# Sharing PSUM banks between a DFT filter and its inverse, and joining eight mixer loops into one, in an fp32 GFNet and MLP-mixer kernel

## The chip, the cores and the metric

The kernel runs on one core of a Trainium2 chip. The metric is the device time of one execution in microseconds. The profile comes from one execution of its own, and its times are read against that execution's span.

## The reference, cut to what matters

The input has 8 batches of 3008 rows by 256 columns, all in fp32. Per batch, a filter in the frequency domain along the rows comes first, then an MLP mixer over the rows (tokens) and one over the columns (channels):

```python
X = np.fft.rfft(x, axis=1)
Y = X * (filt_r + 1j * filt_i)[None, :, :]
x = np.fft.irfft(Y, n=3008, axis=1)
xt = x.transpose(0, 2, 1)
h = np.maximum(xt @ w_tok1, 0.0) @ w_tok2      # 3008 -> 256 -> 3008
u = x + h.transpose(0, 2, 1)
h2 = np.maximum(u @ w_ch1, 0.0) @ w_ch2        # 256 -> 1536 -> 256
out = u + h2
```

## The kernel before, in words

Four stages follow each other for each batch, and stages of different batches run beside each other.

- **Filter, first half** (`a_unit`, lines 376 to 381). The DFT of 3008 = 47 x 64 points is split in two. A unit loads two columns of x, multiplies by a 128x128 table on TensorE (L378), copies the 128x512 result out of PSUM on ScalarE (L380) and stores it to `z_tmp` in device memory (L381). There are 12 units in a batch.
- **Filter, second half** (`b_unit` and `bi_unit`, lines 408 to 444). For each of 32 steps k, `b_unit` multiplies by the second table (L410) into a bank, and VectorE multiplies that bank by the filter (L423, L424, L425 read the bank, L427 adds two products in SBUF). `bi_unit` then applies the inverse table (L434), ScalarE copies the result out (L439), and it is stored to `g_tmp` (L444). In step k the order is: `b_unit(k)`, then `bi_unit(k - 1)`.
- **Token mixer** (`token_sums`, L471; `token_relu`, L477; `u_unit`, L488 to L495). 48 matmuls make the hidden layer of 256. A `u_unit` makes one half of a 512-row tile of u by matmuls with the second weights, adds the end of the inverse DFT (L493), and ScalarE copies it out (L495).
- **Channel mixer** (`mix`, lines 634 to 694). A batch has six row tiles, m, and in each six pairs of hidden blocks, jp: 36 items. The two matrix products use seven block products instead of eight, with sums on VectorE (all recorded on L506). `up_first` (L528, with a ScalarE copy, L531) and `up_last` (L544) make the hidden values in two `pg` banks, VectorE adds them up into hh, ScalarE applies the relu (L549), and `down` in two parts (L562) adds to four banks, po0 to po3. `down` of item i - 1 stands beside `up` of item i. So the loop over a batch has a 37th turn, which has `down` alone. After the last jp of a tile `finish` (lines 565 to 609) gives six steps of VectorE work and stores, which `one_step` takes up one at a time.

PSUM has eight banks: four `po`, two `pg`, and one each named `acc` and `b`. Beside the mixer, `a_unit` and `b_unit` write `b`, and `bi_unit`, `token_sums` and `u_unit` write `acc`. Only in the start, before any mixer runs, are the banks taken differently (`first`).

The order is written out by hand: each engine does its instructions in the order in which the program gives them. `mix` is a generator that stops at three places in each item: after the first part of `down`, place 0; after `up_last`, place 1; and at the item's end, place 2. At these places the loop at lines 733 to 747 puts in one step of `dft`, the filter of the next group of batches. The groups are (0), (1, 2), (3, 4), (5, 6), (7). Beside a group of two batches one step goes in at place 1 of each item. Beside batch 0, which is alone, the 24 first-half units go in at all three places, and the second-half steps at place 1 and in two items of three at place 2. The mixer weights of the channel part are converted on VectorE in the first items of batch 0 (L216 to L242, called by `convert`).

In an item, `u_unit` of the next tile stands at jp 3 and 4, between the second part of `down` and place 2. Near a batch's end (item 32) come the next batch's `token_sums`, then its first two `u_unit`s. `loads` fetches `g_tmp` for the next batch (tile `t4`) when the filter of that batch is done (`next_ready`).

Of the kernel before, what the change touches and what calls it, by code (L numbers as in the profile page):

```python
# [17 lines left out]
B = 8  # L18
# [18 lines left out]
TC = DT // P  # L37
DC = 1536
JT = DC // P
JP = JT // 2  # L40
# [3 lines left out]
MT = 6  # L44
# [73 lines left out]
def kernel(  # L118
# [44 lines left out]

    def bank(tag):
        return (psg if tag == "pg" else psum).tile([P, 512], FP32, tag=tag, name="ps_" + tag)

    wa = glob.tile([P, P], FP32, name="wa")
    wai = glob.tile([P, P], FP32, name="wai")
# [204 lines left out]
    def rows_of(t_d, b):  # L373
        return t_d[b].rearrange("k (g a) d -> (k g) a d", a=A)

    def a_unit(b, c, tag):
        ps = bank(tag)
        nc.tensor.matmul(ps, wa, xs.pop((b, c)).rearrange("p a d -> p (a d)"), start=True, stop=True)  # L378
        t1 = t1p.tile([P, XC, D], FP32, tag="t1", name="t1")
        nc.scalar.copy(out=t1.rearrange("p a d -> p (a d)"), in_=ps)  # L380
        nc.scalar.dma_start(rows_of(z_d, b)[:, ts(c, XC), :], t1)  # L381

    def dft(bs):
        first = bs[0] == 0
        nb = len(bs)
        todo = [(b, c) for b in bs for c in range(NXC)]
        ahead = 3 * XB if first else XB
        for u in todo[0:ahead]:
            x_load(*u)
        for i, u in enumerate(todo):  # L390
            a_unit(*u, ("acc", "b")[i % 2] if first else "b")
            if i + ahead < len(todo):
                x_load(*todo[i + ahead])
            yield i + 1 < len(todo)
        wbs, t2s, t3s, prods = {}, {}, {}, {}

        def load(c):
            if c * KC % WC == 0:
                g = c * KC // WC
                wbs[g] = wbp.tile([P, WC, P + KR], FP32, tag="wb", name="wb")  # L400
                nc.sync.dma_start(wbs[g], wbi_d[:, ts(g, WC), :])
            filt_load(c, (nc.sync, nc.gpsimd, nc.gpsimd) if first else (nc.sync,) * 3)
            where, tag = (sp, "s") if first and c % 3 == 2 else (t2p, "t2")
            t2s[c] = where.tile([KR, KC, nb, D], FP32, tag=tag, name="t2")
            for i, b in enumerate(bs):
                nc.sync.dma_start(t2s[c][:, :, i, :], z_d[b, ts(c, KC)].rearrange("k r d -> r k d"))

        def b_unit(k):
            ps = bank(("b", "pg")[k % 2] if first else "b").rearrange("p (b d) -> p b d", b=2)[:, 0:nb, :]
            nc.tensor.matmul(ps, wbs[k // WC][0:KR, k % WC, 0:P], t2s[k // KC][:, k % KC],  # L410
                             start=True, stop=True)
            re, im = slice(0, HALF), slice(HALF, P)
            t = filts[k // KC % FB]
            fr = t[:, 0, k % KC, :].unsqueeze(1).to_broadcast([P, nb, D])
            fi = t[im, 1, k % KC, :].unsqueeze(1).to_broadcast([HALF, nb, D])
            p1 = p1p.tile([P, 2 if first else nb, D], FP32, tag="p1", name="p1")
            if first:
                p1, p2 = p1[:, 0:1], p1[:, 1:2]
                prods[k] = (p1, p2)
            else:  # L420
                p2 = p2p.tile([P, nb, D], FP32, tag="p2", name="p2")
                prods[k] = (p1,)
            nc.vector.tensor_tensor(out=p1, in0=ps, in1=fr, op=ALU.mult)  # L423
            nc.vector.scalar_tensor_tensor(out=p2[re], in0=ps[im], scalar=-1.0, in1=fi, op0=ALU.mult, op1=ALU.mult)  # L424
            nc.vector.tensor_tensor(out=p2[im], in0=ps[re], in1=fi, op=ALU.mult)  # L425
            if not first:
                nc.vector.tensor_tensor(out=p1, in0=p1, in1=p2, op=ALU.add)  # L427

        def bi_unit(k):

            ps = bank("acc").rearrange("p (b d) -> p b d", b=2)[:, 0:nb, :]
            parts = prods.pop(k)
            for i, p in enumerate(parts):
                nc.tensor.matmul(ps[0:KR], wbs[k // WC][:, k % WC, P:], p, start=(i == 0), stop=(i == len(parts) - 1))  # L434
            c, r = divmod(k, KC)
            if r == 0:
                t3s[c] = t3p.tile([KR, KC, nb, D], FP32, tag="t3", name="t3")

            nc.scalar.copy(out=t3s[c][:, r].rearrange("p b (e g i) -> p b g e i", e=DH, i=CW),  # L439
                           in_=ps[0:KR].rearrange("p b (g e i) -> p b g e i", e=DH, i=CW))  # L440
            if r == KC - 1:
                t3 = t3s.pop(c)
                for i, b in enumerate(bs):
                    nc.scalar.dma_start(g_d[b, ts(c, KC)].rearrange("k r d -> r k d"), t3[:, :, i, :])  # L444

        load(0)
        load(1)
        yield
        yield
        for k in range(K2 + 1):  # L450
            if k < K2:
                b_unit(k)
                if k % KC == 0 and k // KC + 2 < K2 // KC:
                    load(k // KC + 2)
            if k >= 1:
                bi_unit(k - 1)
            yield
# [7 lines left out]
        nc.sync.dma_start(t4[b, c], rows_of(g_d, b)[:, ts(c, TC4), :])  # L465

    def token_sums(b):
        acc = bank("acc").rearrange("p (t d) -> p t d", t=TC)
        for a in range(A):
            for t in range(TC):  # L470
                nc.tensor.matmul(acc[:, t, :], w1[:, a, ts(t, P)], t4[b, a // TC4][:, a % TC4, :],  # L471
                                 start=(a == 0 and t == 0), stop=(a == A - 1 and t == TC - 1))
        return acc
# [9 lines left out]
    def u_unit(b, m, h1, ut, dh):  # L483

        w = width(m)
        ps = bank("acc")
        for t in range(TC):
            nc.tensor.matmul(ps[:, 0:w], h1[:, t, ts(dh, P)], w2[:, t, ds(m * 512, w)],  # L488
                             start=(t == 0), stop=False)
# [138 lines left out]
    todo_v = []  # L628
# [2 lines left out]
        if todo_v:  # L631
            todo_v.pop(0)()

    def mix(b, next_ready):

        wait = [0]
        pos, hhs, tts = {}, {}, {}
        more = b + 1 < B

        def loads():  # L640
            if more and next_ready():
                for c in wait:
                    t4_load(b + 1, c)
                wait.clear()

        items = [(m, jp) for m in range(MT) for jp in range(JP)]
        n = len(items)
        for i in range(n + 1):
            now, old = i < n, i >= 1
            convert()  # L650
            if now:
                m, jp = items[i]
                w = width(m)
                hhs[i] = hp.tile([P, 4, 256], FP32, tag="hh", name="hh")
                g = [bank("pg").rearrange("p (s n) -> p s n", s=2) for _ in range(2)]
                s = up_first(jp, uts[b, m], vts[b, m], w, g)
                up_middle(hhs[i], w, g, s)
            one_step()
            if old:
                mo, jo = items[i - 1]  # L660
                tts[i - 1] = tp.tile([P, 4, 256], FP32, tag="t", name="t")
                for f in h_sums(hhs[i - 1], tts[i - 1], width(mo)):
                    f()
                down(mo, jo, 0, hhs[i - 1], tts[i - 1], pos.setdefault(mo, []))
            yield i, 0
            convert()
            if now:
                up_last(jp, uts[b, m], vts[b, m], w, g, s, hhs[i])
            one_step()
            loads()  # L670
            yield i, 1
            if old:
                down(mo, jo, 1, hhs.pop(i - 1), tts.pop(i - 1), pos[mo])
                if jo == JP - 1:
                    todo_v.extend(finish(b, mo, uts[b, mo], pos[mo]))
                    one_step()
                    one_step()
            if now:
                if m + 1 < MT and jp in (3, 4):
                    u_part(b, m + 1, jp - 3)  # L680
                    if jp == 4:
                        wait.append(m + 1)
                        todo_v.extend(v_steps(b, m + 1))
                if more and i == n - 4:
                    h1s[b + 1] = token_relu(token_sums(b + 1))
                if more and n - 3 <= i < n - 1:
                    u_part(b + 1, 0, i - n + 3)
                    if i == n - 2:
                        todo_v.extend(v_steps(b + 1, 0))
            loads()  # L690
            yield i, 2
        if not more:
            while todo_v:
                one_step()

    with tc.manual_schedule():
        nc.sync.dma_start(wa, wa_d)
# [32 lines left out]
            u_part(0, 0, dh)  # L730
        for f in v_steps(0, 0):
            f()
        for bs, after in zip(GROUPS, GROUPS[1:] + ((),)):
            todo = dft(after) if after else iter(())
            done = not after
            spread = True
            for b in bs:
                def next_ready():
                    return b != bs[-1] or done

                for i, place in mix(b, next_ready):

                    if not done and (place == 1 or bs == GROUPS[0] and (spread or place == 2 and i % 3)):
                        spread = next(todo, "end")
                        done = spread == "end"
            for _ in todo:
                raise AssertionError("the filter's steps don't fit beside the mixer's")


# [28 lines left out]
```

## Time and profile before

| | |
|---|---|
| time, median of three runs | 2620.95 us |
| the three runs | 2620.94, 2620.95, 2629.69 us |
| span of the profiled execution | 2619.4 us (that execution's time: 2621.18 us) |
| mean granted TensorE clock | 0.986 |
| start, before the first channel mixer item | to about 181 us |
| batch 0's mixer, with the filter of batches 1 and 2 beside it | 181 to 557 us |
| a 128x256 matmul of L562, start to start | 0.43 us |
| ScalarE copies of 128x512 | L495 586 ns, L380 572 ns |
| VectorE sum of 128x512 out of PSUM (hh, L506) | 682 ns |

A row of the waits reads: the engine and line that waited, the engine and line that it waited for, the total, how often, and the longest. In the order of time, the number in brackets is how long the engine had been idle, with what ended the idle time. PE is TensorE's matmuls, DVE is VectorE, ACT is ScalarE. An instruction that is recorded as x2 is one fp32 matmul in two records.

### The profile page before, as it was taken

How to read it: one execution, taken by the hardware profiler on the slowest of the kernel's cores; microseconds unless marked ns; L12 is line 12 of the kernel's file. 1: busy time of each engine (PE TensorE's matmuls, PEld its weight loads, DVE VectorE, ACT ScalarE, POOL GpSimd, SP SyncE). 2: the span in 40 equal slices, each digit the busy share in tenths (PEclk: the TensorE clock that was granted, in tenths of full speed). 3: DMA queues.
4: the chain of work that ended last, by engine and by line, in shares of the span. 5: the costliest groups of instructions: out<-in, count | busy, mean ns of one | idle time of the engine just before them, and what ended most of it. 6: DMA issues, size and time to landing. Idle time of an engine off the chain costs nothing.

```text
span 2619.4 us, 31533 instructions
## 1 busy us (share of the span) xinstructions
PE 2513.3 (96%) x10928; PEld 2000.7 (76%) x10928; DVE 1804.4 (69%) x3461; ACT 678.9 (26%) x1325; POOL 519.3 (20%) x951
## 2 busy tenths in 40 slices
PE   6869999999999999999999999999999999999998
PEld 2446666788878777888787777788888888888887
DVE  3787788645666888646567688745678586647676
ACT  2223222222321222213222222212222122212222
POOL 3534111211121111211212111121121121211212
PEclk7879999999999999999999999999999999999999
DMA  8765433312232332202332222211322111100001
GB/s 235 221 192 177 123 111 111 103 42 89 85 100 63 88 89 61 87 9 90 95 101 85 74 82 75 75 33 56 95 77 84 54 46 55 25 9 8 17 10 22
DMA packets 158104, 212.89 MB, mean 81 GB/s; under 512 B 35012, under 2 KB 106383, under 8 KB 157945
## 3 DMA queue, kind: packets, MB, share of 16 engines
q1 hardware_dynamic: 85897, 120.34, 15.7%
q0 software_dynamic: 30656, 39.92, 6.2%
q10 hardware_dynamic: 41392, 50.62, 5.7%
q8 instruction: 86, 1.41, 0.2%
q14 instruction: 73, 0.60, 0.1%
HBM read 135.77 MB, written 74.97 MB: 80 GB/s over the span
## 4 chain that ended last, share of the span: by engine, by line
PE 74%; DVE 14%; issue 2%; ACT 1%; DMA 0%; DVEq 0%; SPq 0%; POOL 0%; ACTq 0%; POOLq 0%
PE ps_po L562 26%; PE ps_pg L528 15%; PE ps_pg L544 11%; PE ps_acc L488 6%; PE ps_acc L471 6%; PE ps_acc L493 3%; DVE t L506 3%; DVE hh L506 3%; PE ps_b L410 3%; PE ps_b L378 2%; PE ps_acc L434 2%; DVE u L506 2%; DVE s L506 1%; DVE p L425 1%; DVE p L424 1%
## 5 line engine op out<-in xcount | busy, mean ns | idle before, releaser
L506 DVE TENSOR_TENSOR hh<-ps_pg,s 128x512 f32<-128x512 f32 (+3 forms) x864 | 482.8, 586 | 643.8 <-ACT s L531 643.2
L607 POOL DMA_DIRECT2D out_dram<-r x757 | 409.8, 550 | 1964.7 <-ACT hh L549 893.9
L549 ACT ACTIVATE hh<-hh 128x512 f32<-128x512 f32 (+1 forms) x576 | 348.0, 621 | 1103.0 <-DVE hh L506 1103.0
L562 PE MATMUL ps_po<-t,wc 128*128 128x256 f32 (+1 forms) x2304 | 535.5, 375 | 3.5 <-DVE t L506 2.2
L562 PEld LDWEIGHTS ps_po<-t,wc 128*128 128x128 f32 x2304 | 434.4, 190 | 127.6 <-issue 50.8
L562 PE MATMUL ps_po<-hh,wc 128*128 128x256 f32 (+1 forms) x1728 | 413.1, 375 | 3.1 <-ACT hh L549 3.1
L528 PE MATMUL ps_pg<-v,wc 128*128 128x256 f32 (+1 forms) x1728 | 414.1, 376 | 1.6 <-DVE v L506 1.6
L562 PEld LDWEIGHTS ps_po<-hh,wc 128*128 128x128 f32 x1728 | 327.4, 190 | 42.4 <-ACT hh L549 5.1
L528 PEld LDWEIGHTS ps_pg<-v,wc 128*128 128x128 f32 x1728 | 327.6, 190 | 41.7 <-DVE v L506 2.3
L544 PE MATMUL ps_pg<-u,wc 128*128 128x256 f32 (+1 forms) x1152 | 294.1, 378 | 9.6 <-DVE hh L506 9.3
L506 DVE TENSOR_TENSOR t<-t,hh 128x256 f32<-128x256 f32 (+1 forms) x576 | 242.9, 422 | 19.8
L544 PEld LDWEIGHTS ps_pg<-u,wc 128*128 128x128 f32 x1152 | 215.3, 190 | 49.2 <-DVE hh L506 22.3
L506 DVE TENSOR_TENSOR s<-ps_pg,hh 128x512 f32<-128x512 f32 (+1 forms) x288 | 196.1, 681 | 30.6 <-DVE hh L506 0.5
L506 DVE TENSOR_TENSOR t<-hh 128x512 f32<-128x512 f32 (+1 forms) x288 | 192.5, 668 | 0.6 <-ACT hh L549 0.6
L488 PE MATMUL ps_acc<-w,h 128*128 128x512 f32 (+1 forms) x384 | 181.7, 596 | 7.7 <-ACT h L477 3.5
L471 PE MATMUL ps_acc<-t,w 128*128 128x256 f32 x768 | 170.3, 384 | 8.0 <-DMA t<-g_tmp 6.7
L528 PE MATMUL ps_pg<-u,wc 128*128 128x256 f32 (+1 forms) x576 | 170.3, 377 | 0.4 <-DVE hh L506 0.4
L471 PEld LDWEIGHTS ps_acc<-t,w 128*128 128x128 f32 x768 | 147.5, 193 | 29.8 <-issue 7.1
L544 PE MATMUL ps_pg<-v,wc 128*128 128x256 f32 (+1 forms) x576 | 168.9, 375 | 0.0
L410 PE MATMUL ps_b<-t,wb 96*128 96x512 f32 (+1 forms) x288 | 130.3, 533 | 31.8 <-DMA t<-z_tmp 17.6
L434 PE MATMUL ps_acc<-p,wb 128*96 128x256 f32 (+1 forms) x384 | 154.7, 497 | 2.4 <-DVE p L423 1.1
L531 ACT COPY s<-ps_pg 128x256 f32<-128x256 f32 (+1 forms) x288 | 106.0, 368 | 152.0 <-PE ps_pg L528 147.4
(71 smaller groups left out, 1954.2 us busy)
## 6 DMA issues: line engine op xcount, KB each, us to landing
z_tmp<-t ACTq DMA_DIRECT2D x96, 256.0 KB
t<-z_tmp SPq DMA_DIRECT2D x128, 192.0 KB
g_tmp<-t ACTq DMA_DIRECT2D x128, 192.0 KB
t<-g_tmp SPq DMA_DIRECT2D x48, 512.0 KB
x<-in_x_dram SPq DMA_DIRECT2D x184, 128.0 KB
out_dram<-r POOLq DMA_DIRECT2D x698, 32.0 KB, 1.8
wb<-wbi_t SPq DMA_DIRECT2D x80, 224.0 KB
filt<-in_filt_r_dram SPq DMA_DIRECT2D x144, 48.0 KB
```

Of the source, the lines that this page charges most:

```text
L410: nc.tensor.matmul(ps, wbs[k // WC][0:KR, k % WC, 0:P], t2s[k // KC][:, k % KC], start=True, stop=True)
L434: nc.tensor.matmul(ps[0:KR], wbs[k // WC][:, k % WC, P:], p, start=(i == 0), stop=(i == len(parts) - 1))
L471: nc.tensor.matmul(acc[:, t, :], w1[:, a, ts(t, P)], t4[b, a // TC4][:, a % TC4, :], start=(a == 0 and t == 0), stop=(a == A - 1 and t == ...
L488: nc.tensor.matmul(ps[:, 0:w], h1[:, t, ts(dh, P)], w2[:, t, ds(m * 512, w)], start=(t == 0), stop=False)
L493: nc.tensor.matmul(ps[:, ds(q * P, n)], t4[b, c][:, r, ts(dh, P)], wai[:, 0:n], start=False, stop=(q == 3))
L506: nc.vector.tensor_tensor(out=out, in0=in0, in1=in1, op=op)
L528: nc.tensor.matmul(ps[:, 0:hw], wc1[:, jp, n, :], mov, start=True, stop=True)
L531: nc.scalar.copy(out=s[:, 0], in_=g[0][:, 0, 0:hw])
L544: nc.tensor.matmul(ps[:, 0:hw], wc1[:, jp, n, :], mov, start=True, stop=True)
L549: nc.scalar.activation(out=hs, in_=hs, func=AF.Relu)
L562: nc.tensor.matmul(po[i][:, j, 0:hw], wc2[:, jp, n, :], mov, start=(jp == 0 and first == 1), stop=(jp == JP - 1 and last == 1))
L607: q.dma_start(rows[g, e, :, ds(h * A + 4 * m, n)], blocks[ts(g, CW), h, e, 0:n])
```

## The change

It has two parts.

**Banks.** A helper `free_bank` gives acc and b in turn, except that it passes over a bank that is held. `a_unit`, `token_sums` and `u_unit` all take their bank from it. Beside the mixer `b_unit(k)` takes its bank from it too and holds it; `bi_unit(k)` writes its result into the same bank, over the product that VectorE has read by then, and the hold ends. So the product and the inverse of one step share a bank, and at most one bank is held while something else asks. In the start `b_unit` and `bi_unit` keep their banks, while `a_unit`, `token_sums` and `u_unit` take turns there too.

**One sequence.** `mix` runs once over 288 items of all eight batches, not eight times over 36. The 37th turn of seven batches goes: `down` of a batch's last item stands beside `up` of the next batch's first item. The loop at the end becomes one loop, which starts the next group's `dft` when the first item of a group is reached.

The diff, cut to its core:

```diff
+    turn, held = ["acc", "b"], []
+
+    def free_bank():
+        turn.reverse()
+        if turn[0] in held:
+            turn.reverse()
+        return turn[0]
...
-    def a_unit(b, c, tag):
-        ps = bank(tag)
+    def a_unit(b, c):
+        ps = bank(free_bank())
...
-            a_unit(*u, ("acc", "b")[i % 2] if first else "b")
+            a_unit(*u)
...
-            ps = bank(("b", "pg")[k % 2] if first else "b").rearrange("p (b d) -> p b d", b=2)[:, 0:nb, :]
+            tag = ("b", "pg")[k % 2] if first else free_bank()
+            if not first:
+                held.append(tag)
+            ps = bank(tag).rearrange("p (b d) -> p b d", b=2)[:, 0:nb, :]
...
-            ps = bank("acc").rearrange("p (b d) -> p b d", b=2)[:, 0:nb, :]
+            ps = bank("acc" if first else held.pop(0)).rearrange("p (b d) -> p b d", b=2)[:, 0:nb, :]
...
-        acc = bank("acc").rearrange("p (t d) -> p t d", t=TC)
+        acc = bank(free_bank()).rearrange("p (t d) -> p t d", t=TC)
...
-        ps = bank("acc")
+        ps = bank(free_bank())
...
-    def mix(b, next_ready):
-
-        wait = [0]
+    def mix(next_ready):
+
+        wait = []
...
-        items = [(m, jp) for m in range(MT) for jp in range(JP)]
-        n = len(items)
-        for i in range(n + 1):
-            now, old = i < n, i >= 1
+        items = [(b, m, jp) for b in range(B) for m in range(MT) for jp in range(JP)]
+        n = MT * JP
+        for i in range(len(items) + 1):
+            now, old = i < len(items), i >= 1
             convert()
             if now:
-                m, jp = items[i]
+                b, m, jp = items[i]
+                if i % n == 0:
+                    wait.append(0)
...
-        for bs, after in zip(GROUPS, GROUPS[1:] + ((),)):
-            todo = dft(after) if after else iter(())
...
-                for i, place in mix(b, next_ready):
-
-                    if not done and (place == 1 or bs == GROUPS[0] and (spread or place == 2 and i % 3)):
-                        spread = next(todo, "end")
-                        done = spread == "end"
...
+        for b, i, place in mix(next_ready):
+            if group + 1 < len(GROUPS) and b == GROUPS[group + 1][0]:
+                if not done:
+                    raise AssertionError("the filter's steps don't fit beside the mixer's")
+                group += 1
+                done = group + 1 == len(GROUPS)
+                todo = iter(()) if done else dft(GROUPS[group + 1])
+                spread = True
+
+            if not done and (place == 1 or group == 0 and (spread or place == 2 and i % 3)):
+                spread = next(todo, "end")
+                done = spread == "end"
```

## The prediction

> **What bounds the kernel now.** First the page's span and busy times, then the busy times by stage. The columns of the second view are the stretch and its length, busy us and instructions of each engine, granted TensorE clock, DMA share and GB/s; the stages are the start, the mixer of batch 0 up to 453 us, the steady part, the end.
>
> ```profile
> span 2619.4 us, 31533 instructions
> PE 2513.3 (96%) x10928; PEld 2000.7 (76%) x10928; DVE 1804.4 (69%) x3461; ACT 678.9 (26%) x1325; POOL 519.3 (20%) x951
> ```
>
> ```profile
> 0.00:167.00 167.00, 121.02 (x360) 69.93 (x360) 107.37 (x233) 42.79 (x86) 70.91 (x133) 0.85 0.80 234
> 167.00:453.00 286.00, 257.03 (x980) 179.37 (x981) 231.32 (x410) 81.70 (x152) 64.64 (x109) 0.97 0.43 128
> 453.00:2566.00 2113.00, 2092.63 (x9372) 1711.28 (x9371) 1429.72 (x2745) 542.92 (x1064) 372.39 (x688) 1.00 0.22 64
> 2566.00:2620.00 54.00, 42.61 (x219) 40.14 (x217) 35.96 (x75) 11.46 (x24) 11.39 (x21) 0.94 0.09 19
> ```
>
> TensorE is the bound, and no matmul is added or removed, so only its idle time and its half clock can go: 46 us in the start, 29 in batch 0's mixer, 20.4 in 2113 us of the steady part, 11.4 at the end. The waits of TensorE (total us, times, longest) name the owners that the change touches:
>
> ```profile
> PE ps_b L410 <- DVE p L425: 14.0, 9, 1.8
> PE ps_b L378 <- ACT t L380: 11.7, 5, 4.1
> PE ps_pg L544 <- DVE hh L506: 9.3, 15, 1.9
> PE ps_po L562 <- ACT hh L549: 3.1, 5, 0.7
> ```
>
> All nine waits of the first row lie between 305 and 467 us, beside batch 0's mixer, where two filter steps follow each other with only L562 between. In time order (idle before an instruction in brackets):
>
> ```profile
> 369.93 0.56 ACT L439 COPY t<-ps_acc 96x512 f32<-96x512 f32 x1
> 371.49 0.68 DVE L425 TENSOR_TENSOR p<-ps_b,filt 64x512 f32<-64x512 f32 x1
> 372.20 0.69 DVE L427 TENSOR_TENSOR p<-p,p 128x512 f32<-128x512 f32 x1
> 372.23 1.13 PE L410 MATMUL ps_b<-t,wb 96*128 96x512 f32 x2 [1.55 <-DVE p L425]
> ...
> 193.51 1.65 PE L378 MATMUL ps_b<-x,wa 128*128 128x512 f32 x2 [4.08 <-ACT t L380]
> ...
> 197.31 0.42 DVE L506 TENSOR_TENSOR hh<-ps_pg,s 128x256 f32<-128x256 f32 x1 [1.81 <-ACT s L531]
> ...
> 558.24 1.40 PE L562 MATMUL ps_po<-hh,wc 128*128 128x224 f32 x6 [0.75 <-ACT hh L549]
> ...
> 870.83 1.13 PE L544 MATMUL ps_pg<-u,wc 128*128 128x256 f32 x4 [1.91 <-DVE hh L506]
> ```
>
> The last two are ends of a batch: the extra turn of the loop has `down` without `up` beside it.
>
> **What the Trainium skill says.** "PSUM — Partial Sum Buffer", section "PSUM bank collisions raise a hardware error": guard PSUM by bank, not by address. The trace agrees: L410 at 372.23 starts 0.06 us after L425, the bank's last reader, ended. Same page, "Engine vs sequencer instructions": ScalarE and VectorE take their queues strictly in order. It agrees: a copy (L380) whose matmul ended at 189.43 runs at 192.89, behind two relus (L549, from 191.76). "TensorE: Matmul & The Clock Gate", "What's actually happening": after an idle window of about 3.4 us the clock is halved. It agrees: from 190.57 to 193.98 TensorE is busy 0.47 us, and the next 3.42 us have a granted clock of 0.50.
>
> **Part 1, token product's bank and first u bank (start).** The two `u_unit`s of batch 0, both in acc before, now take acc and b. The wait L488 <- ACT u L495 of 0.73 us at 175.78 goes; the clock there is half until 180.33, so some of the work that moves up runs slower. I take **0.5** (0 to 0.7). It counts, as VectorE idles 3.94 us until 181.92 for this u.
>
> **Part 2, 24 `a_unit`s beside batch 0 (181 to 271).** They took b alone, now acc and b in turn. Waits L378 <- ACT L380 there: 4.08 + 2.06 + 0.48 = 6.6 us (the other 5.1 of the row are in the start, where the banks alternated already), and 1.7 us are lost to the half clock after the first. But the next matmuls, L528, need the pg banks that VectorE releases (hs sums, 191.04 to 192.32), and VectorE, with the weights' conversion (L216 to L242, some 3 us each), is then the bound: its idle time from 189 to 221 is 1.81 + 0.36 at 197, 0.95 at 208, 0.96 at 220, no more. So the gain is what VectorE idles, **4.1**. Lower bound 2: loads of x, two buffers deep, took some 6 us from issue (207.8) to use (214.15), and two of the waits beside these are for x (1.71, 1.18). Upper bound 8.3, were TensorE's own idle and clock all that counted.
>
> **Part 3, filter and inverse in one bank, group 0 (275 to 490).** L410 of step k+1 no longer waits for L425 of step k; it takes the bank that L439 cleared. In the piece above that copy ends at 370.49, TensorE is free at 370.67: no wait. But behind L410 stands L434 of step k, which needs L427, 0.7 us later than L425. L427 ends at 372.89; L434 starts then at about 372.93, before it was 373.19: of 1.55 us only 0.26 come back; the wait moves to L434. VectorE gains the 0.49 us that it idled for L410 each time, yet the next u2 sum waits for L531 on ScalarE, so again about 0.25; every third time VectorE bounds and 0.5 come back. Nine times: 3 x (0.26 + 0.25 + 0.49) = 3.0 gained.
> A wait is added: where `u_unit` stands just ahead of a second filter step (once in six items), u takes the only bank that isn't held, and L410 must wait for u's copy, L495. At 425.82 L410 started as u's last matmul ended; the copy ran from 426.02 to 426.61, so it starts at 426.66: +0.84, with L434 and all of TensorE's queue behind it, and VectorE's products too. Three times: 2.5 lost (bounds 0 to 3.5). The last inverse, which waited 0.62 for a u copy in acc at 490.35, waits no more. Sum **1.1** gained (-1 to 3).
> From group 1 on a step comes once an item (some 8 us), and L439 or L495 are over several us earlier; I cost the shared bank there at nothing, hidden behind the 14 mixer matmuls. `token_sums` takes the bank that L439 is emptying, as before (waits L471 and L488 <- ACT L439, 2.7 us together, stay).
>
> **Part 4, one sequence of mixers.** At seven batch ends the last `down` now lies between the next batch's L528, L544 and the filter's matmuls. Idle there before, by boundary (us): 557: 0.75 + 0.21; 868: 1.97; 1172: 0.95; 1483: 1.97; 1786: 0.95; 2089: 1.30; 2362: 1.39. Sum 9.5. Behind: L528 of the next batch needs v (done 558.4 in pieces, its first at 557.9) and pg banks (557.6); relu of the last item ended at 558.19, before L562 now comes. What stays: a tile's end inside a batch, the same order of work, idles 0.3 to 0.5 with filter steps (802.56: 0.33, 810.18: 0.21) and about 0.1 without. 3 x 0.35 + 4 x 0.05 = 1.2. Gain **8.3** (6.5 to 9.5). `finish` has two of its steps an item as inside a batch; loads of t4 and x keep their order on SP's queue, stores theirs on POOL's; filter steps lose the extra turn (37 of a batch, now 36), and 59 of them stand before 72 places, so they are done in time.
>
> **Sum.** 0.5 + 4.1 + 1.1 + 8.3 = 14.0 of the span 2619.4, to 2605.4. The runs shown are 2620.94, 2620.95 and 2629.69; the median is 1.55 over the span. 2620.95 - 14.0 = **2607**.
>
> **Rivals.** *Only the batch ends pay*: x loads and VectorE take back what the second bank gives beside batch 0, and the u wait eats part 3: 8.3 + 0.5 + 2 - 1, some 10: **2611**. For it: 0.81 of VectorE's time is busy there; against: VectorE's idle does come from TensorE. *TensorE counts in full beside batch 0*: part 2 gives 8.3, **2603**; for it the half clock after the 4.08 wait, against it VectorE's short idle time. *Slower*: the pair holds a bank until L439 has emptied it, and L439 stands behind the relus on ScalarE; were the bank not free at the next L410 in the steady part, each of 96 steps there would stall. It decides from 14.0 / 96 = 0.15 us each; at 0.3 each it is +28.8 - 14.0, **2636**. Against it: with steps 8 us apart the copy ends about 3 us after its matmul (390.64 after 387.64), over 4 us early. *Nothing changes* because banks aren't what the built order waits for: 2621; against it, the built order has the last `down` inside the next item at all seven ends.
>
> **How the numbers follow.** Forecast 0.58, only the batch ends 0.25, TensorE in full 0.13, slower 0.02, nothing 0.02. 0.5% is 13.1 us, about what a measurement of this kernel can tell from no change, so the line lies at 2607.85: of the forecast's 0.58, 0.42 lie below it; with 0.13 that is faster 0.55. Same: 0.16 + 0.25 + 0.02 = 0.43. Slower 0.02. The parts' bounds and the two rivals next to the forecast give 2602 to 2612 for 8 in 10.
>
> **What would show it.** Right: the row L410 <- DVE L425 gone, a row L434 <- DVE p L427 of some 12 us in its place, a row L410 <- ACT u L495 of about 2.5; L378 <- ACT L380 down to some 5; the steady part's idle time from 20.4 to about 12, with no wait of 0.7 or 1.9 at a batch end. Wrong: bank waits on ACT L439 from group 1 on; DMA x waits that grow as L378's shrink; VectorE idle as before between 189 and 221.

## The result and the profile after

The changed kernel takes 2603.85 us in the median of four runs (2602.21 to 2605.86), the kernel before 2621.26 beside it: ratio 0.9926, interval 0.9905 to 0.9948. Two repeats on the chip gave 0.9938 (0.9924 to 0.9951) and 0.9930 (0.9917 to 0.9942). So it is faster by some 17 us, where 14 were forecast. That the total came so near is in part luck: it hides two larger errors that go opposite ways, some 6 us too little at the batch ends and 4 us too much for the first-half units, and they are what this part is about.

First the page's span and busy times, then the busy times by stage, as for the kernel before (the last two stretches are set so that they hold the same instructions as before).

```profile
span 2603.4 us, 31550 instructions
PE 2509.6 (96%) x10928; PEld 2000.1 (77%) x10928; DVE 1806.2 (69%) x3461; ACT 678.2 (26%) x1325; POOL 521.6 (20%) x951
```

```profile
0.00:167.00 167.00, 122.08 (x360) 70.14 (x360) 105.18 (x228) 42.46 (x85) 70.03 (x131) 0.84 0.79 229
167.00:453.00 286.00, 256.21 (x980) 177.83 (x981) 236.10 (x415) 82.20 (x152) 66.37 (x112) 0.98 0.44 131
453.00:2550.00 2097.00, 2088.80 (x9372) 1712.03 (x9371) 1428.92 (x2745) 542.08 (x1064) 373.72 (x688) 1.00 0.22 65
2550.00:2604.00 54.00, 42.55 (x219) 40.14 (x217) 35.95 (x75) 11.46 (x24) 11.43 (x21) 0.94 0.09 19
```

The steady part has the same 9372 matmul records and is 16.0 us shorter. TensorE's idle time in it fell from 20.4 to 8.2 us. Its busy time fell too, from 2092.6 to 2088.8, though the work is the same: this is the first thing to explain.

The waits of TensorE (total us, times, longest):

```profile
PE ps_acc L448 <- DVE p L440: 5.6, 6, 1.1
PE ps_acc L388 <- ACT t L390: 4.3, 3, 3.2
PE ps_b L448 <- DVE p L440: 3.9, 3, 1.3
PE ps_pg L558 <- DVE hh L520: 2.7, 9, 0.4
PE ps_b L388 <- ACT t L390: 2.1, 3, 0.9
PE ps_acc L423 <- ACT u L509: 2.0, 3, 0.7
```

The lines have moved by 10 to 14: L448 is the inverse (L434 before), L423 the product (L410), L388 the first half (L378), L576 is `down` (L562). The product no longer waits for VectorE; the inverse does, for its own product, 9 times. L388's waits for the copy are all in the start. No long wait of a batch end is left.

Where the time went, from profiled executions. The columns are us, worked out from the starts of L528's first matmul of an item in the trace: from the end of the first token sums (relu) to the second u copy; batch 0's first to ninth item; ninth to 31st; 31st to the last matmul.

| kernel | first u copies | items 1 to 9 | items 9 to 31 | item 31 to the end |
|---|---|---|---|---|
| before | 14.15 | 89.07 | 228.05 | 2110.6 |
| before, second profile | 14.39 | 88.60 | 229.14 | 2110.6 |
| after | 11.36 | 88.93 | 227.20 | 2096.2 |
| after, second profile | 11.61 | 89.45 | 227.19 | 2096.8 |
| after, third profile | 11.16 | 91.03 | 227.26 | 2096.9 |
| sequence alone | 12.28 | 93.18 | 228.15 | 2096.1 |
| banks alone | 11.23 | 89.23 | 227.19 | 2111.2 |

In the first pair of profiles that is -2.8, -0.1, -0.9 and -14.4, against gains of 0.5, 4.1, 1.1 and 8.3 forecast. The first token sums themselves ended 2.2 us later in the profile after, which brings the 18.2 to the 16.0 by which the spans differ. Over all runs that point lies anywhere from 164.6 to 170.6 us, and the two kinds of kernel overlap in it.

### The profile page after: what moved, and what is told of

It is laid out like the page before. It is cut to its first block, busy times and chain, and to the rows that moved or that the text cites. A ratio compares the mean times of both kernels' runs of the same rounds, so it can differ in the third digit from the quotient of the medians.

```text
span 2603.4 us, 31550 instructions
## 1 busy us (share of the span) xinstructions
PE 2509.6 (96%) x10928; PEld 2000.1 (77%) x10928; DVE 1806.2 (69%) x3461; ACT 678.2 (26%) x1325; POOL 521.6 (20%) x951
## 4 chain that ended last, share of the span: by engine, by line
PE 81%; DVE 11%; DMA 3%; issue 2%; ACT 1%; SPq 1%; POOL 0%; ACTq 0%; DVEq 0%; POOLq 0%
PE ps_po L576 29%; PE ps_pg L542 16%; PE ps_pg L558 12%; PE ps_b L485 3%; PE ps_acc L502 3%; PE ps_b L502 3%; PE ps_acc L485 2%; PE ps_acc L448 2%; DVE t L520 2%; DVE hh L520 2%; PE ps_acc L507 2%; PE ps_b L507 2%; PE ps_b L423 2%; PE ps_acc L423 1%; PE ps_b L448 1%
## 5 line engine op out<-in xcount | busy, mean ns | idle before, releaser
L563 ACT ACTIVATE hh<-hh 128x512 f32<-128x512 f32 (+1 forms) x576 | 347.8, 621 | 1112.2 <-DVE hh L520 1112.2
L576 PE MATMUL ps_po<-t,wc 128*128 128x256 f32 (+1 forms) x2304 | 535.4, 375 | 3.6 <-DVE t L520 2.2
L576 PEld LDWEIGHTS ps_po<-t,wc 128*128 128x128 f32 x2304 | 434.5, 190 | 130.2 <-issue 53.1
L542 PE MATMUL ps_pg<-v,wc 128*128 128x256 f32 (+1 forms) x1728 | 414.2, 376 | 3.2 <-POOL wc L314 3.0
L576 PE MATMUL ps_po<-hh,wc 128*128 128x256 f32 (+1 forms) x1728 | 413.0, 375 | 0.4 <-POOL wc L315 0.3
L542 PEld LDWEIGHTS ps_pg<-v,wc 128*128 128x128 f32 x1728 | 326.8, 190 | 44.2 <-DVE v L520 3.9
L576 PEld LDWEIGHTS ps_po<-hh,wc 128*128 128x128 f32 x1728 | 327.5, 190 | 39.2 <-ACT s L545 1.2
L520 DVE TENSOR_TENSOR t<-t,hh 128x256 f32<-128x256 f32 (+1 forms) x576 | 243.3, 422 | 19.8
L558 PEld LDWEIGHTS ps_pg<-u,wc 128*128 128x128 f32 x1152 | 215.5, 190 | 41.3 <-DVE hh L520 14.8
L542 PE MATMUL ps_pg<-u,wc 128*128 128x256 f32 (+1 forms) x576 | 170.0, 377 | 1.4 <-DVE hh L520 1.3
L558 PEld LDWEIGHTS ps_pg<-v,wc 128*128 128x128 f32 x576 | 108.6, 190 | 13.2
L542 PEld LDWEIGHTS ps_pg<-u,wc 128*128 128x128 f32 x576 | 102.5, 191 | 20.4 <-issue 9.2
L485 PE MATMUL ps_b<-t,w 128*128 128x256 f32 x480 | 106.8, 385 | 8.2 <-DMA t<-g_tmp 7.2
L485 PEld LDWEIGHTS ps_b<-t,w 128*128 128x128 f32 x480 | 92.5, 193 | 22.1 <-DMA t<-g_tmp 7.6
L448 PE MATMUL ps_acc<-p,wb 128*96 128x256 f32 (+1 forms) x256 | 96.2, 477 | 7.3 <-DVE p L440 5.6
```

The source lines that it names most:

```text
L520: nc.vector.tensor_tensor(out=out, in0=in0, in1=in1, op=op)
L542: nc.tensor.matmul(ps[:, 0:hw], wc1[:, jp, n, :], mov, start=True, stop=True)
L558: nc.tensor.matmul(ps[:, 0:hw], wc1[:, jp, n, :], mov, start=True, stop=True)
L563: nc.scalar.activation(out=hs, in_=hs, func=AF.Relu)
L576: nc.tensor.matmul(po[i][:, j, 0:hw], wc2[:, jp, n, :], mov, start=(jp == 0 and first == 1), stop=(jp == JP - 1 and last == 1))
```

## The experiments

Each is told with its edit, what was expected, and what came.

**The sequence alone, and the banks alone.** The first is the changed kernel with its joined loop, and every bank as before:

```diff
-    def a_unit(b, c):
-        ps = bank(free_bank())
+    def a_unit(b, c, tag):
+        ps = bank(tag)
...
-            a_unit(*u)
+            a_unit(*u, ("acc", "b")[i % 2] if first else "b")
...
-            tag = ("b", "pg")[k % 2] if first else free_bank()
-            if not first:
-                held.append(tag)
+            tag = ("b", "pg")[k % 2] if first else "b"
...
-            ps = bank("acc" if first else held.pop(0)).rearrange("p (b d) -> p b d", b=2)[:, 0:nb, :]
+            ps = bank("acc").rearrange("p (b d) -> p b d", b=2)[:, 0:nb, :]
...
-        acc = bank(free_bank()).rearrange("p (t d) -> p t d", t=TC)
+        acc = bank("acc").rearrange("p (t d) -> p t d", t=TC)
...
-        ps = bank(free_bank())
+        ps = bank("acc")
```

The second is the kernel before with `free_bank` and every line that uses it put in, and a mixer for each batch.

> One sequence of mixers alone, all banks as before. Theory 1 (a wait costs more than the idle time shown for it: from start to start some 0.27 us more each, and the seven batch ends hold about 14 waits): some 13 to 14.5 us faster, about 2607, and the shift of the last matmul against before comes in seven steps of about 1.1 (ends without filter steps) and 3 (ends with them). Theory 2 (the ends are worth the idle time shown, as predicted, 8.3 us, and the rest of the measured gain comes from the banks): about 2613, and 1 to 2 us a step.

> The bank edits alone, eight mixers one after the other. Theory 1: 1 to 4 us faster, about 2618, nearly all of it before batch 0's first mixer item and in the filter's last step; no gain over the 24 first-half units beside batch 0. Theory 2: 5 to 9 us faster, about 2614, most of it over the first-half units.

On one chip the kernel before took 2624.11 us (21 runs), the sequence alone 2608.92 (ratio 0.9946, 0.9933 to 0.9958), the banks alone 2618.65 (0.9979, 0.9971 to 0.9986). So the sequence is worth 15.2 us and the banks 5.5 (by size in theory 2's range, but not where theory 2 put it). The trace puts the sequence's part at 14.5 us from item 31 to the end (table: 2110.6 to 2096.1), in steps, from one end to the next, of 1.1 to 1.6 for the ends without filter steps and 2.8 to 3.5 for those with them: theory 1's sizes. The banks gain nothing there (2111.2). Their 5.5 isn't found in the profile of that run: in its four stretches they gain 2.9, -0.2, 0.9 and -0.6 us against the kernel before. The two together, 20.7, are also more than the 17 of the whole change; the intervals, some 3 us wide to either side for the first and 2 for the second, allow for both.

Why did 9.5 us of idle time at batch ends turn into 14.5? Look at how long a wait is from start to start. TensorE before, in time order, at the end without filter steps at 557 us, and at the one with them at 868:

```profile
555.80 1.70 PE L562 MATMUL ps_po<-t,wc 128*128 128x224 f32 x8
...
867.46 1.46 PE L528 MATMUL ps_pg<-v,wc 128*128 128x256 f32 x6
```

and the same places in the changed kernel:

```profile
554.19 1.70 PE L576 MATMUL ps_po<-t,wc 128*128 128x224 f32 x8
555.72 0.59 PE L542 MATMUL ps_pg<-u,wc 128*128 128x256 f32 x2
...
859.99 1.46 PE L542 MATMUL ps_pg<-v,wc 128*128 128x256 f32 x6
861.28 1.30 PE L576 MATMUL ps_po<-hh,wc 128*128 128x224 f32 x6
862.42 1.03 PE L558 MATMUL ps_pg<-u,wc 128*128 128x256 f32 x4
```

Without a wait, six records of L542 are followed by the next matmul 1.29 us after their start (859.99 to 861.28), although the row says that they took 1.46: the last record's end is modelled 0.17 us past the point at which the next one can start. Before, L528 started at 867.46 and its successor, L544, at 870.83 (the prediction shows that row): 3.37 - 1.29 = 2.08 us lost, where the idle time shown is 1.91. And the four records after the wait took 1.13 us, here 1.03: another 0.10. At 555.80 likewise: the next start was due 1.53 us later, as after (554.19 to 555.72), and came at 558.24, 0.91 late, for an idle time of 0.75; and the six records took 1.40, not 1.30. **A wait costs 0.27 us more than the idle time shown**, and a wait below 0.17 isn't shown at all. Reckoned in the same way, from the starts of all matmuls, the other waits of the steady part cost 0.24 to 0.27 more than shown. That fits the 3.8 us of "busy" time that went: 14 x 0.27 is 3.8. The seven ends held 14 waits: 9.5 + 14 x 0.27 = 13.3.

Next comes a wait that the prediction had kept. `u_unit` waited for the copy L439 (ScalarE) at 1053.70, 1668.03 and 2160.59, 0.50, 0.50 and 0.37 us as shown, 2.2 with the hidden part. With one turn less the filter's steps stand one item later against the end of a batch, and the wait is gone, with the banks as before too: the sequence alone has no such row. So 15.5 were there to be had. The new ends aren't free of waits: eight are shown in them, of 0.04 to 0.13 us, 0.6 in all, and at the same price they cost some 2.7. (In the rows above, L542 at 556.35 starts 0.63 us after 555.72, where 0.43 was due.) That leaves 12.8 of the 14.5. The other 1.7 are spread over short delays within the batches and were not placed one by one.

**The first-half units' second bank.** Here 4.1 us were forecast, and the first pair of profiles shows nothing. One run kept the joined loop and the second bank for these units, and had every other bank as before; against the sequence alone its edit is:

```diff
-            a_unit(*u, ("acc", "b")[i % 2] if first else "b")
+            a_unit(*u, ("acc", "b")[i % 2])
```

> One sequence, and of the bank edits only that the first-half units beside the mixer take acc and b in turn; product in b, inverse, token sums and u in acc as before. Theory 1 (what the second bank gives TensorE is used up by VectorE, which runs longer beside GpSimd): within 1.5 us of the sequence alone, with VectorE's busy time from batch 0's first item to its fifth about 3 us more than before. Theory 2: 4 us faster than the sequence alone.

It took 2614.26 us (0.9968, 0.9955 to 0.9981), 5.3 more than the sequence alone on the same chip, and items 1 to 9 took 93.36: the time misses both theories. As units took acc by their number, they met the u units there: u waited 2.3 us for a unit's copy at 227.5, and a unit 0.8 for u's at 243.9. It isn't a clean test of the second bank. The next four runs compare the kernels before and after.

> The kernel before, looked at again. Theory 1 (what one bank costs the first-half units beside batch 0 depends on the clock: a wait of 2 to 4 us halves the clock in one or two of the next 3.4 us windows, by the window's place in time): from the first to the ninth item of batch 0, 89 to 94 us (89.1 in the first profile of this kernel, 93.2 with the sequence alone, which has the same banks there), with one to three stretches of half clock after 181 us. Theory 2 (the first profile is what the kernel always does): 89.1 within 0.5.

> The changed kernel again, in more rounds. Theory 1: 88.5 to 89.3 us from the first to the ninth item of batch 0, as in the three profiles so far with these banks (88.9, 89.2, 88.7); the last matmul's time against the first item of batch 1 as before within 0.3 us; some 18 to 20 us faster than the kernel before by the medians (the sequence's 15.2 and the banks' 5.5 measured apart on one chip, less 1 to 2). Theory 2: 16 to 17 us.

The second profiles (table) gave 88.60 before and 89.45 after. By the runs the changed kernel was 16.8 us faster, as theory 2 had it: what the two halves gave apart, 20.7, doesn't come back in full. The kernel before varied little here, against theory 1, but the sequence alone, with the same bank for these units, took 93.18 with 10.2 us of half clock after 190 us, against 3.4 in both profiles before. The changed kernel's third profile had 91.03 with one such stretch more than its first; its second had two more and yet 89.45. So half clock explains only a part of the scatter. A wait can halve TensorE's clock in the next stretch, by where it lies in time. The clearest case is the banks alone at a batch end, a wait of 2.07 us at 866.37. Columns as in the stages:

```profile
866.20:869.60 3.40, 1.33 (x6) 1.04 (x6) 3.30 (x9) 0.47 (x2) 0.00 (x0) 1.00 0.48 124
869.60:873.10 3.50, 3.50 (x6) 1.50 (x5) 3.04 (x6) 1.23 (x2) 0.00 (x0) 0.51 0.08 9
```

TensorE is busy 1.33 of 3.40 us, and the next stretch runs at half clock. The same wait in the kernel before, 1.91 shown from 868.92, did not. The stretches of half clock in that trace begin at 193.98 and 2614.03, which are 709 stretches of 3.413 us apart; counted on from there, the wait falls across two of them, and TensorE is busy for most of each:

```profile
866.41:869.82 3.41, 2.51 (x13) 1.95 (x11) 3.36 (x7) 0.72 (x2) 0.00 (x0) 1.00 0.80 233
869.82:873.23 3.41, 2.40 (x9) 1.72 (x10) 3.31 (x9) 0.42 (x1) 0.00 (x0) 1.00 0.13 35
```

So the price of a long wait has a second part, 0 or some 1.7 us (estimated: half of a stretch); at this end the banks alone fell 1.5 us behind the kernel before.

Last, what holds the units if not the bank. From batch 0's first item to its ninth VectorE does the same 123 instructions in both kernels. It idles less in the changed kernel, 18.2 us against 21.5, a little less than forecast, but it is busy longer, 70.8 us against 67.6 (70.7 against 67.5 in the second profiles). Groups of VectorE's instructions by form between 181 and 235 us (times, busy us, mean ns), before and then after:

```profile
L216 DVE TENSOR_SCALAR top<-top 128x512 uint32<-128x512 uint32 x9 | 4.0, 442 | 0.0
L506 DVE TENSOR_TENSOR t<-t,hh 128x256 f32<-128x256 f32 x6 | 3.8, 629 | 0.2
```

```profile
L226 DVE TENSOR_SCALAR top<-top 128x512 uint32<-128x512 uint32 x9 | 5.6, 617 | 0.0
L520 DVE TENSOR_TENSOR t<-t,hh 128x256 f32<-128x256 f32 x7 | 4.7, 677 | 0.2
```

A sum of two SBUF tiles took 425 ns elsewhere. GpSimd combines the converted mixer weights in the same stretch (L311 to L315). The Trainium skill, "SBUF — State Buffer", section "Who interferes with whom", says that a VectorE instruction with two SBUF inputs contends with a GpSimd instruction that reads SBUF, since the second input comes over a shared interface. Two runs leave the combining out. The slots that it fills hold zeros there, so the combined weights are missing from the result; the matmuls are the same in number and size:

```diff
     def combine(w):
-        a11, a12, s4, na22, s3, s2, s1 = (w[:, :, n, :] for n in range(7))
...
+        return
...
         nc.sync.dma_start(wa, wa_d)
+        nc.gpsimd.memset(wc1, 0.0)
+        nc.gpsimd.memset(wc2, 0.0)
```

> The kernel before without GpSimd's combining of the mixer weights (L301 to L305; the slots that it would write hold zeros). Theory 1 (VectorE's sums with two inputs in SBUF run longer beside GpSimd's combining): no sum t of 128x256 near 0.77 us in the first items, all near 0.43, and VectorE 2 to 3 us less busy between 181 and 235; the time from the first to the ninth item 86 to 92, TensorE's waits for the one bank staying (4.0 and 2.0 us). Rival (the longer sums come from DMA traffic or from the clock): sums of 0.77 us stay.

> The changed kernel without GpSimd's combining of the mixer weights (L311 to L315; zeros in their place). Theory 1 (what the second bank frees is used up by VectorE, which in the changed kernel spends 3.3 us more on the same sums because they now lie beside the combining): 85 to 87 us from the first to the ninth item, 2 to 4 less than the 88.9 with it, and 3 or more below the kernel before in the same form. Rival (loads of x bind): 88.5 or more, and waits for x as long as with it (6.3 us in all).

The changed kernel's VectorE without the combining, same stretch:

```profile
L226 DVE TENSOR_SCALAR top<-top 128x512 uint32<-128x512 uint32 x10 | 4.2, 421 | 0.0
L514 DVE TENSOR_TENSOR t<-t,hh 128x256 f32<-128x256 f32 x8 | 3.4, 425 | 0.3
```

These sums are back at 425, in the kernel before too, so the combining lengthens them, not the DMA traffic or the clock. Items 1 to 9 took 87.78 us before and **83.87** after, less than the 85 to 87 expected; VectorE is busy 64.0 us in both and idles 23.8 and 19.8. So with GpSimd out of the way the changed kernel is 3.9 us shorter here, near the 4.1 forecast; with GpSimd there, the profiles of the two kernels show no gain. This rests on one profile of each, and up to 1.7 of the 3.9 may be the clock: the kernel before had two stretches of half clock, the changed one one. The one time of each, 2620.48 and 2598.48 us, differs by 22, where the kernels with the combining differ by 17.

The pair shows that the combining takes away what the second bank gives. It doesn't show by which way, since more goes with the combining than the longer sums. TensorE's waits from 178 to 272 us, before and then after, both with the combining:

```profile
PE ps_b L378 <- ACT t L380: 6.6, 3, 4.1
PE ps_b L378 <- DMA x<-in_x_dram: 3.2, 4, 1.7
```

```profile
PE ps_acc L388 <- DMA x<-in_x_dram: 3.3, 3, 1.3
PE ps_acc L388 <- ACT hh L563: 3.0, 1, 3.0
PE ps_pg L542 <- POOL wc L314: 3.0, 1, 3.0
PE ps_b L388 <- DMA x<-in_x_dram: 0.7, 1, 0.7
```

The units' waits for the copy are gone. In their place TensorE waits in the first item for GpSimd itself, for a combined weight (L314; 2.7 and 3.3 us in the other two profiles). Its first matmul with v comes 3.6 us after the item's start, where it was 2.2. And the waits for x grew, which the prediction had named as a sign of being wrong: 3.2 and 3.5 us in the two profiles before, some 7.0, 5.6 and 8.9 in the three after. (The 7.0 count in the wait put down to the relu L563, which doesn't touch that bank; the third profile has a wait for x in that place, 2.85 at 216.6.) Without the combining they are 2.9 before and 3.2 after. So longer sums, combined weights that come late, and loads of x all stand for the 4.1 that didn't come, and their shares stay open.

**A remedy for that, and one for the double steps.** The first moves one of the five combining steps:

```diff
-        nc.gpsimd.tensor_scalar(out=na22, in0=s1, scalar1=-1.0, scalar2=None, op0=ALU.mult)
+        nc.scalar.activation(out=na22, in_=s1, func=AF.Copy, scale=-1.0)
```

> The changed kernel with one of the five steps of combining the mixer weights, the negation at L311, on ScalarE in place of GpSimd. If VectorE's longer sums beside GpSimd bind batch 0's first items: GpSimd has some 0.55 to 0.85 us less per tile, nine tiles, and the time from the first to the ninth item falls by 0.5 to 1.5 us from 88.9. Rival: GpSimd's next step then waits for ScalarE, whose queue has the relus ahead, and the time grows by 1 to 3 us.

It took 2606.32 us; the changed kernel on the same chip, run a third time, 2606.54.

> The changed kernel on the same chip as the two others, to hold them against: 88.5 to 89.5 us from the first to the ninth item, 227.2 from there to the 31st, and 0.8% or less under the kernel before.

From the first item to the ninth VectorE was busy 67.5 us in place of 70.8, as little as in the kernel before, and TensorE's wait for L314 is gone. But these items took 89.32: waits of 2.1 and 2.6 us for VectorE and 4.9 in all for x stand there, and two stretches of half clock after 188 us. So VectorE's longer busy time alone isn't what holds the units. The third profile of the changed kernel itself missed its expectation by 1.5 us in items 1 to 9, with a stretch of half clock at 225.9.

The second chooses other items for the second filter step:

```diff
-            if not done and (place == 1 or group == 0 and (spread or place == 2 and i % 3)):
+            if not done and (place == 1 or group == 0 and (spread or place == 2 and i % 6 in (0, 2, 3, 4))):
```

> The changed kernel with the second filter step beside batch 0 in items 0, 2, 3 and 4 of six (after both u units, and two more), not 1, 2, 4, 5. The wait of an inverse for its own product (L448 on VectorE's L440) is about 1.5 us from start to start where two steps follow each other directly, and about 0.9 (for u's copy) where a u unit lies between. If that is the remaining price of the double steps: 0.5 us saved in each of three and a half tiles, 1 to 2.5 us faster than the changed kernel, about 2602. If VectorE's total work bounds batch 0's mixer: no difference.

Items 9 to 31 took 226.59 us against 227.20: 0.6 saved, where 1 to 2.5 were expected for the whole, and 2604.45 us is no measurable gain. Both together:

> Both: the negation on ScalarE, and the second filter step in items 0, 2, 3 and 4 of six. The effects add: 0.6 us less from the ninth to the 31st item, as in the kernel with the other items alone, and the same from the first to the ninth item as with the negation alone. By the clock 1 to 2 us below the changed kernel, which the rounds can hardly tell from nothing.

It took 2603.77 us, 2.8 under the changed kernel on the same chip, with 88.44 and 226.46 us in the two stretches. The second is as expected; the first is 0.9 below the negation alone, which is within the scatter of the profiles. By the runs (0.9926, 0.9914 to 0.9938, beside 0.9930, 0.9917 to 0.9942) it can't be told from the changed kernel.

## Why the prediction was right or wrong, step by step

**Part 4, the batch ends, was mis-sized: 8.3 forecast, 14.4 measured.** The mechanism held, all seven ends closed. The step that failed is the price: idle time as shown was taken as what a wait costs. Each of the 14 waits cost 0.27 us more (3.8 us in all); the same holds for the 1.2 us taken off for waits inside the new ends, of which 0.6 is shown and some 2.7 was paid. Second, the three waits of `u_unit` for L439, 2.2 us, were said to stay; the filter's shift by one turn removed them. That accounts for 12.8; the other 1.6 lie in short delays within the batches, which the term left out.

**Part 2, the second bank for the first-half units, was mis-sized the other way: 4.1 forecast, 0 measured.** The step that failed is "the gain is what VectorE idles". VectorE's idle time did fall, by 3.3 us, but its busy time rose by 3.2: the term took the durations of VectorE's sums as fixed, while they depend on what GpSimd does beside them. It also left out that the first item waits for the combined weights, and it took growing waits for x into its lower bound alone. Without the combining 3.9 are there. Which of the three holds how much is open.

**Part 3 held: 1.1 forecast, 0.9 measured** (1.9 in the second profiles). The wait moved from product to inverse as worked out; in time order, after:

```profile
372.33 0.69 DVE L440 TENSOR_TENSOR p<-p,p 128x512 f32<-128x512 f32 x1
373.07 1.10 PE L448 MATMUL ps_b<-p,wb 128*96 128x512 f32 x2 [1.29 <-DVE p L440]
...
425.89 1.12 PE L423 MATMUL ps_acc<-t,wb 96*128 96x512 f32 x2 [0.68 <-ACT u L509]
```

L448 starts 0.05 us after L440 has ended. The added wait for u's copy is shown as 0.68, three times (2.0 against "about 2.5"); with the hidden 0.17 that is close to the 0.84 forecast. L448's own waits are 9.5 us as shown, where some 12 were named.

**Part 1's stretch is 2.8 us shorter, where 0.5 was forecast**, but it isn't shown that this is the bank's doing. The wait of 0.73 went, and the half clock over these matmuls lasted 6.8 us, not 13.7. The sequence alone, with the old banks there, had 10.2 us of half clock and was 1.9 shorter. And the first item starts at 181.1 and 178.2 us in the two profiles before, at 180.5, 176.6 and 180.7 in the three after: a gain by then isn't shown beyond the scatter.

**The rivals.** "Only the batch ends pay" was right in place and wrong in size: in the profile they gave 14.4 of 16.0 us. Its reason, that the loads of x and VectorE take back what the second bank gives, fits the profiles. "TensorE counts in full" named the half clock, which did matter, but its 8.3 for part 2 did not come. The slower rival needed waits on L439 from group 1 on: there are none beyond those at the token sums (1.3 us, as before).

## What to carry to other kernels

Price a wait of TensorE from start to start, against the same matmuls without a wait, not by the idle time shown; here 14 waits of 9.5 us as shown weighed 13.3. Where a step is to be gained from an engine's idle time, ask which of its instructions will come to lie beside another engine's work that lengthens them, and which wait stands right behind the one that goes. Moving the last step of a pipelined loop into the next loop's first paid once for each end, and it moved everything that was placed by counting turns as well.

## What the runs showed that was not expected

Half clock at a wait was a matter of place: 2.07 us idle in the banks alone, all in one stretch, brought 3.4 us at 0.51; 1.91 us at the same matmuls in the kernel before, across two stretches, brought none. And VectorE's one-input conversion step on 128x512 words (L226), no two-input sum, also ran longer beside GpSimd: 617 ns in the mean, 421 without the combining.
